# Attention with a relative bias, then routed experts: one PSUM ring for bias and scores, and a new order of the work

## The chip, the cores and the metric

The kernel runs on one core of a Trainium2 chip. The metric is the device time of one execution in microseconds; before, the median of three runs is 383.62 us (377.87, 383.62 and 387.02). Engines: PE (TensorE) multiplies matrices into PSUM, ACT (ScalarE) and DVE (VectorE) work on elements, POOL (GpSimd) and SP (SyncE) here mostly issue DMAs. [...]

## The reference

Eight batches, eight heads, 576 positions, head size 64; then eight experts over the 4608 resulting rows of 512.

```python
scores = scale * np.matmul(q, k.transpose(0, 1, 3, 2))
x = (psi_rel / psi_i)[..., None]          # psi_rel = log1p(|i - j|), psi_i = log1p(max(i, 1))
h = np.maximum(x @ w1 + b1, 0.0)          # hidden size 32
bias = h @ w2                             # one value for each head, i and j
scores = scores + bias.transpose(2, 0, 1)[None, :, :, :]
attn = np.exp(scores - max); attn = attn / sum
x = np.matmul(attn, v)                    # rows of all heads side by side
for e in range(E):
    mask = domain_id == e
    out[mask] = np.maximum(x[mask] @ w1[e], 0.0) @ w2[e]
```

## The kernel before, in words

The kernel has three stages.

**Bias.** The bias is the same in every batch, so the exponential of it is computed once and kept in SBUF (`biasM`, `biasR`, `biasL`, `biasRL`), and the exponentials of the scores are multiplied by it. `_phase_bias` goes through nine groups of 16 hidden rows. `hidden(ib)` makes the rows `hr`, some on ACT (L205), the others on DVE (L208); `outputs(ib, hrl)` multiplies them by the second layer into a PSUM tile `eb` (L225, and L229 for the last 64 keys), and ACT takes the exponential (L241, L238, L248). The ninth group (ib 8) is for the last 64 queries. Between these the routing (`_phase_route`, a generator of small DVE instructions) and the first transposes of q and k are woven in.

**Attention.** `_Attention.run` goes through nine rounds of 21 units; round b computes the scores of batch b (`scores`: score matmuls L530, L536, L543, L552 into a PSUM tile `sc`; exponential on ACT, L556) and the sums over the values (`av`, L580 to L596, into `pu`) of batch b and of what is left of batch b - 1. `weight` multiplies by the bias on DVE (L567), `norm` divides (L610, L611; L623, L627 for the last 64 positions) and scatters rows to `x_dram` on POOL's queue, at positions that the routing gave. `PLAN` is the written order: A is `av`, N `norm`, W `weight`, T and D transposes of q and k for the next batch on PE (L480) and their copy by DVE (L505), V the values with a column of ones; a prime means the batch before. PE, DVE and ACT keep the written order (`manual_schedule`); DMAs on POOL's queue keep theirs through `G.issue`.

PSUM: two banks `tr` for transposes and the routing, for the whole kernel; in the bias stage three `eb` tiles of two banks; in attention two `sc` tiles of two banks and one accumulator `pu` of two banks; with the experts two `hps` tiles of two banks and two `ops` tiles of one.

**Experts.** `_phase_moe`: for each expert the rows are fetched from `x_dram` by a transposing DMA (`fetch`, three tiles in turn), `first` computes the hidden layer (L781, relu on ACT, L813), `second` the output in five chunks of 128 rows (L757, copied by DVE, L760, and scattered by POOL, L761). The first 512 rows of expert 0 (`EARLY`) are fetched in the last attention round. Weights are loaded in 32 parts by POOL (L719): 17 during attention, and 15 one after each chunk. `_phase_overflow` is a loop over chunks that had no room in an expert's 640 rows; it stands behind everything and runs no time with these inputs.

## Time and profile before

| what | value |
|---|---|
| median of three runs | 383.62 us |
| span of the profiled execution | 383.4 us |
| PE busy over the span | 330.1 us (86%) |
| DVE busy | 238.8 us (62%) |
| ACT busy | 248.8 us (65%) |
| first score exponential | at 56.80 us |
| first matmul of the experts | at 229.16 us |
| issue of the last scatter | 373.92 to 374.90 us |

The shares over the whole span mix the three stages, so the stretches are to be read one by one. A row of a group gives line, engine, operation, output and input, shape and count, busy time and mean length of one, and then how long the engine had been idle before them and what ended it. "remote" stands where nothing that the profile shows ended an idle time. [...]

### The profile page before, as it was taken

How to read it: one execution, taken by the hardware profiler on the slowest of the kernel's cores; microseconds unless marked ns; L12 is line 12 of the kernel's file. 1: busy time of each engine (PE TensorE's matmuls, PEld its weight loads, DVE VectorE, ACT ScalarE, POOL GpSimd, SP SyncE). 2: the span in 40 equal slices, each digit the busy share in tenths (PEclk: the TensorE clock that was granted, in tenths of full speed). 3: DMA queues.
4: the chain of work that ended last, by engine and by line, in shares of the span. 5: the costliest groups of instructions: out<-in, count | busy, mean ns of one | idle time of the engine just before them, and what ended most of it. 6: DMA issues, size and time to landing. Idle time of an engine off the chain costs nothing. (4 is left out here: it accounts for less than half of the span.)

```text
span 383.4 us, 9399 instructions
## 1 busy us (share of the span) xinstructions
PE 330.1 (86%) x3938; PEld 216.2 (56%) x3938; DVE 238.8 (62%) x456; ACT 248.8 (65%) x303; POOL 177.3 (46%) x220
## 2 busy tenths in 40 slices
PE   1489997779898989989897779999999996999990
PEld 0378774546565665656574554665565644565630
DVE  7999968999899999999999762202122121212030
ACT  8999968789899989899989834242332402231500
POOL 9250006109486766676964513737451064233241
PEclk9999757999999999999999989999999998999996
DMA  5999977909999998979999933999999997021221
GB/s 87 179 172 370 374 276 98 146 0 129 130 150 152 130 169 106 181 103 200 132 210 227 229 76 82 200 238 205 237 206 231 185 181 224 28 93 56 77 89 39
DMA packets 90995, 61.30 MB, mean 160 GB/s; under 512 B 43461, under 2 KB 85189, under 8 KB 90952
## 3 DMA queue, kind: packets, MB, share of 16 engines
q0 software_dynamic: 59904, 45.12, 69.9%
q1 hardware_dynamic: 31048, 15.57, 17.0%
q8 instruction: 31, 0.51, 0.5%
q14 instruction: 12, 0.10, 0.1%
HBM read 61.93 MB, written 24.70 MB: 226 GB/s over the span
## 5 line engine op out<-in xcount | busy, mean ns | idle before, releaser
L556 ACT ACTIVATE e<-sc 128x1024 f16<-128x1024 f32 x168 | 152.8, 1012 | 16.2 <-PE sc L530 12.8
L760 DVE COPY res<-ops 128x512 f32<-128x512 f32 x40 | 27.7, 692 | 114.2 <-PE ops L757 108.2
L813 ACT ACTIVATE hT<-hps 128x640 f16<-128x640 f32 x56 | 39.4, 703 | 83.1 <-PE hps L781 77.8
L567 DVE TENSOR_TENSOR e<-e,biasM 128x2048 f16<-128x2048 f16 x64 | 71.8, 1151 | 1.8 <-ACT e L556 1.4
L757 PE MATMUL ops<-w,hT 128*128 128x512 f16 x320 | 70.5, 379 | 0.0
L761 POOL DMA_INDIRECT out_dram<-res,ids x40 | 39.7, 992 | 62.5 <-DVE res L760 48.5
L781 PE MATMUL hps<-xT,w 128*128 128x320 f16 x448 | 64.0, 304 | 3.0 <-ACT hT L813 3.0
L530 PE MATMUL sc<-qkT 64*128 64x512 f16 x256 | 49.9, 394 | 9.9 <-ACT e L556 8.0
L781 PEld LDWEIGHTS <-w 128*128 128x128 f16 x448 | 44.5, 99 | 22.4 <-issue 3.4
L757 PEld LDWEIGHTS <-hT 128*128 128x128 f16 x320 | 31.2, 98 | 36.5 <-ACT hT L793 0.3
L584 PE MATMUL pu<-vext,e 128*128 128x65 f16 x1024 | 50.1, 196 | 0.0
L641 POOL DMA_INDIRECT fire_x<-xt,posi x32 | 38.7, 1210 | 22.8 <-DMA last<-in_q_dram 10.3
L584 PEld LDWEIGHTS <-e 128*128 128x128 f16 x1024 | 44.4, 100 | 3.3 <-issue 2.4
L719 POOL DMA_DIRECT2D w<-in_moe_w_dram x32 | 28.1, 905 | 30.0 <-PE hps L781 18.6
L208 DVE TENSOR_SCALAR hr<-L,slope,nb 128x576 f16<-128x576 f16 x116 | 41.3, 450 | 0.0
L225 PE MATMUL eb<-W2BIG,hr 128*128 128x32 f16 x576 | 27.9, 193 | 13.1 <-DVE hr L208 9.4
L580 PE MATMUL pu<-vrag,e 128*128 128x130 f16 x128 | 29.2, 228 | 7.4 <-DVE xt L611 6.1
L225 PEld LDWEIGHTS <-hr 128*128 128x128 f16 x576 | 23.3, 116 | 17.6 <-DVE hr L208 14.4
L641 POOL DMA_INDIRECT fire_x<-xl,posi x8 | 13.3, 1667 | 39.3 <-DVE vext L477 18.6
L530 PEld LDWEIGHTS <-qkT 64*128 64x128 f16 x256 | 15.0, 93 | 25.4 <-issue 15.7
L580 PEld LDWEIGHTS <-e 128*128 128x128 f16 x128 | 12.6, 98 | 21.9 <-issue 10.1
L505 DVE COPY qkT<-pt 128x1024 f16<-128x1024 f16 x32 | 22.0, 688 | 4.3 <-PE pt L480 4.3
(124 smaller groups left out, 372.7 us busy)
## 6 DMA issues: line engine op xcount, KB each, us to landing
w<-in_moe_w_dram POOLq DMA_DIRECT2D x32, 512.0 KB
fire_x<-zero SPq DMA_DIRECT2D x1, 9252.0 KB
qn<-in_q_dram POOLq DMA_DIRECT2D x8, 512.0 KB
kn<-in_k_dram POOLq DMA_DIRECT2D x8, 512.0 KB
vst<-in_v_dram POOLq DMA_DIRECT2D x8, 512.0 KB
out_dram<-res,ids POOLq DMA_INDIRECT x40
last<-zero SPq DMA_DIRECT2D x2, 256.0 KB, 3.3
last<-in_q_dram POOLq DMA_DIRECT2D x16, 32.0 KB
```

The lines of the kernel that those rows point to most:

```text
L208: nc.vector.tensor_scalar(out=hr, in0=G.L4[:, c0: c0 + S], scalar1=G.slope[:, m: m + 1], scalar2=G.nb1[:], op0=AO.mult, op1=AO.max)
L225: nc.tensor.matmul(out=eb[:, lj, 32 * k16: 32 * k16 + 32], lhsT=rap(hr, jc, [[4, 128]]), rhs=G.W2BIG[:, 0:32], start=True, stop=True)
L530: mm(out=sc[:, h2, :], lhsT=self.qkT[b, p][hs[h2], 1, 128 * c: 128 * c + 128], rhs=self.qkT[b, p][hs[h2], 0, :], start=not raw, stop=True)
L556: nc.scalar.activation(out=ef[:, 0:n], in_=sf[:, 0:n], func=AF.Exp, bias=0.0, scale=0.125)
L567: self.nc.vector.tensor_tensor(out=job[0], in0=job[0], in1=job[1], op=AO.mult)
L580: mm(out=self.pu[:, c // 2, o: o + 130], lhsT=er[:, p % 2, 128 * c: 128 * c + 128], rhs=vr[:, p, :], start=True, stop=False, skip_group_ch ...
L584: mm(out=self.pu[:, c // 2, o + 65 * h2: o + 65 * h2 + 65], lhsT=self.e[b, ("m", p, j)][:, h2, 128 * c: 128 * c + 128], rhs=vx[:, 2 * p + ...
L641: inst = self.nc.gpsimd.indirect_dma_start(out=self.x_dram[:, :], out_offset=bass.IndirectOffsetOnAxis(ap=self.G.posi[0:n, c:c + 1], axis= ...
L757: nc.tensor.matmul(out=ops_, lhsT=hT[:, fc, t0: t0 + 128], rhs=G.w.w2(e, fc), start=(fc == 0), stop=(fc == 7))
L761: inst = nc.gpsimd.indirect_dma_start(out=out[:], out_offset=bass.IndirectOffsetOnAxis(ap=idx.bitcast(I32), axis=0), in_=res[:], in_offset ...
L781: nc.tensor.matmul(out=hps[:, i, 0:HC], lhsT=G.w.w1(e, dc, fc), rhs=xT[:, dc, HC * hf: HC * hf + HC], start=(dc == 0), stop=(dc == 3))
L813: nc.scalar.activation(out=hT[:, fc, :].rearrange("p (a b) -> p a b", a=2), in_=first(e, xT, ((fc, 0), (fc, 1))), func=AF.Relu, bias=0.0, ...
```

## The change

One PSUM pool serves bias and attention: a ring of three tiles of two banks, used by the bias outputs, the scores and the pairs of transposes, and one tile `pu` of two banks, which the accumulators, the routing and the first transposes share. The transposes are made for two pairs of heads at once and copied by one instruction; one such copy, that of pairs 2 and 3 for batch 1, is done by ACT.

```diff
+            aps = att.enter_context(tc.tile_pool(name="aps", bufs=1, space=PS, reuse_waits="tile"))
+            G.ring = lambda: aps.tile([P, 2, 512], F32, tag="sc", name="sc", bufs=3)
+            G.acc = lambda: aps.tile([P, 2, 512], F32, tag="pu", name="pu", bufs=1)
...
-        sc = G.aps.tile([P, 2, 512], F32, tag="sc", name="sc", bufs=2)
+        sc = G.ring()
...
-            eb = fps.tile([P, 2, 512], F32, tag="eb", name="eb", bufs=3)
+            eb = G.ring()
...
+            o, i = t.rearrange("p i x f -> p i (x f)"), self.pt.pop((b, ps)).bitcast(F16)
+            if (b, ps) == (1, (2, 3)):
+                self.nc.scalar.copy(out=o, in_=i)
+            else:
+                self.nc.vector.tensor_copy(out=o, in_=i)
```

The plan by units is replaced by a list that orders units, sums, copies and multiplications alike. The bias becomes a generator: its last group's three outputs come after the score units `m03`, `m10` and `m11` of batch 0 (`LAST_ROWS`), and the unit `m00` of each batch is put into the round before.

```diff
+ROUND = """
+V r0 m01 N2' A40' A41' Wm31' Wm32' A42' A43' N4'
+m02 m03 A30' A31' Wr0 A32' A33' m10 m11 Wm01 N3'
+T01 Wm03 m12 m13 A00 A01 D01 m20 m21 Wm11 A02
+A03 Wm13 m22 N0 Wm21 m23 T23 r1 D23 A10 l0
+A11 l1 A12 A13 m30 x Wm23 m31 Wr1 N1 A20
+Wl1 A21 m00+ A22 D4 A23 m32 Wx m33
+""".split()
+LAST_ROWS = {"m03": 1, "m10": 1, "m11": 2}
```

In the bias the last 64 keys are written into both halves of the partitions by two matmuls for each row, of 16 columns each, so that one exponential on 128 partitions takes the place of two on 64. ACT makes three hidden rows in each group from the third on (before three or two), and one table set that holds the logarithm and the exponential is loaded at the start. `W2BIG` and `vrag` are cleared in front of the first slopes, and the second half of the logarithms (`rest`) comes after the first hidden rows.

```diff
-                    for h2 in range(2):
-                        o = G.biasR[64 * h2: 64 * h2 + 64, :, i0: i0 + 64] if ib < 8 else \
-                            G.biasRL[64 * h2: 64 * h2 + 64]
-                        nc.scalar.activation(out=o, in_=ebv[0:64, 0, h2::2, :],
-                                             func=AF.Exp, bias=0.0, scale=0.125)
+                        for h2 in range(2):
+                            nc.tensor.matmul(out=eb[64 * h2: 64 * h2 + 64, 0, 16 * k16: 16 * k16 + 16],
                                              lhsT=hr[:, 512:576],
+                                             rhs=rap(G.W2BIG, h2, [[2, 16]]), start=True, stop=True)
...
+                nc.scalar.activation(out=G.biasR[:, :, i0: i0 + 64] if ib < 8 else G.biasRL,
+                                     in_=eb[:, 0, 0:256].rearrange("p (i q) -> p q i", q=4),
+                                     func=AF.Exp, bias=0.0, scale=0.125)
...
+    nc.scalar.add_instruction(mybir.InstLoadActFuncSet(
+        name=nc.get_next_instruction_name(), engine=mybir.EngineType.Activation, act_func_set_id=LN_EXP,
+        ins=[], outs=[]))
```

The routing has some instructions fewer. The sums of the last 64 positions go to 128 partitions (two halves of a row each), so that one normalisation takes the place of two, and half rows are scattered; a row of `x_dram` is now two halves of 256 values, each with its own row number. Of a batch's row scatters, one goes out at once and three after later units (`send`); in the last two batches all four.

Weights: 19 parts are loaded during attention (four after one unit of batch 0), the other 13 in four bunches after experts 1 to 4. All experts' rows are fetched at the start of the expert stage, into eight tiles. PSUM of the experts is laid over the ring and the accumulator as four pools of two banks, with four `ops` tiles. The last pair of heads of the last batch accumulates in two ring tiles. The last chunk's output is made and copied in two halves, one by DVE and one by ACT. The overflow loop moves in front of the last expert, behind a condition.

```diff
+W_FIRST = {0: 4, 1: 2, 2: 2, 3: 2, 4: 1, 5: 1}
+W_LATE = {1: 3, 2: 4, 3: 3, 4: 3}
...
-    xTs = {e: fetch(e) for e in range(2)}
+    xTs = {e: fetch(e) for e in range(E)}
+    novf = None
     for e in range(E):
+        if e == E - 2:
+            novf = nc.values_load(G.novf[0:1, 0:1], min_val=0, max_val=NOVF)
+        if e == E - 1:
+            with tc.If(novf > 0):
+                _phase_overflow(tc, G, novf, moe_w1, moe_w2, x_dram, out)
...
         for kk in range(NCH):
-            if (e, kk) == (0, 2):
+            if (e, kk) == (0, 3):
                 first_rest(hT, xT)
             second(hT, 128 * kk, e, ids[:, kk, :])
-            G.w.load(1, G.w_late)
+        G.w.load(W_LATE.get(e, 0), G.w_first)
...
-    _phase_overflow(tc, G, moe_w1, moe_w2, x_dram, out)
...
+        ops, hps = cycle((0, 0, 2, 2)), cycle((1, 3))
+        G.ops = lambda: pools[next(ops)].tile([P, DM], F32, tag="ops", name="ops", bufs=2)
+        G.hps = lambda shape, dt=F32: pools[next(hps)].tile(shape, dt, tag="hps", name="hps")
...
+                if (b, p) == (B - 1, 3) and c % 2 == 0:
+                    self.pu = G.ring()
```

## Rows read from the trace of the kernel before

**Rows 1.** The first line of the page.
```profile
span 383.4 us, 9399 instructions
```

**Rows 2.** Stretches: us, length, busy time (instructions) by engine, clock, DMA share, GB/s.
```profile
0.00:56.80 56.80, 39.97 (x766) 34.09 (x766) 50.77 (x159) 51.47 (x74) 17.17 (x38) 0.87 1.06 246
56.80:81.50 24.70, 19.08 (x278) 12.35 (x277) 22.52 (x45) 19.30 (x21) 7.59 (x12) 0.87 0.74 95
81.50:204.00 122.50, 110.95 (x1793) 75.93 (x1791) 116.62 (x175) 114.39 (x127) 85.58 (x100) 1.00 1.00 145
204.00:225.60 21.60, 17.78 (x239) 11.90 (x238) 17.13 (x26) 19.14 (x22) 9.22 (x10) 0.92 0.99 195
225.60:229.20 3.60, 1.60 (x40) 1.38 (x38) 1.82 (x6) 0.00 (x0) 0.91 (x1) 1.00 0.36 81
229.20:374.90 145.70, 140.72 (x836) 80.50 (x832) 29.93 (x48) 44.48 (x61) 56.83 (x59) 0.99 0.77 155
```
The engines stand in the order PE, PEld, DVE, ACT, POOL.

**Rows 3.** The same view of two stretches with another granted clock.
```profile
42.60:59.50 16.90, 15.82 (x262) 12.25 (x264) 12.75 (x35) 13.50 (x21) 0.00 (x0) 0.50 0.76 274
...
322.50:325.80 3.30, 3.30 (x14) 1.88 (x13) 0.00 (x0) 1.41 (x2) 0.00 (x0) 0.50 0.34 72
```

**Rows 4.** Timeline of ACT and of DVE at the hand-over to attention: start, length, instruction.
```profile
53.74 2.21 ACT L248 ACTIVATE biasL<-eb 128x512 f16<-128x512 f32 x4 [2.95 <-PE eb L225]
...
58.35 0.69 DVE L505 COPY qkT<-pt 128x1024 f16<-128x1024 f16 x1 [4.15 <-PE pt L480]
```

**Rows 5.** Groups by line, 81.5 to 204 us: count, busy, mean ns, idle before.
```profile
L556 ACT ACTIVATE e<-sc 128x1024 f16<-128x1024 f32 (+1 forms) x127 | 115.4, 1013 | 8.1 <-PE sc L530 6.6 <-PE sc L536 0.6
...
L530 PE MATMUL sc<-qkT 64*128 64x512 f16 x192 | 36.5, 383 | 5.4 <-ACT e L556 4.3
```

**Rows 6.** Groups by line and shape, whole span.
```profile
L556 ACT ACTIVATE e<-sc 128x1024 f16<-128x1024 f32 x160 | 150.6, 1042 | 16.2 <-PE sc L530 12.8 <-PE sc L536 1.5 <-PE sc L543 0.7
...
L567 DVE TENSOR_TENSOR e<-e,biasM 128x2048 f16<-128x2048 f16 x56 | 67.0, 1217 | 1.8 <-ACT e L556 1.4 <-issue 0.2
...
L208 DVE TENSOR_SCALAR hr<-L,slope,nb 128x576 f16<-128x576 f16 x116 | 41.3, 450 | 0.0
...
L205 ACT ACTIVATE hr<-L,pb,slope 128x576 f16<-128x576 f16 x28 | 22.2, 858 | 1.0 <-DVE slope L169 0.8
L505 DVE COPY qkT<-pt 128x1024 f16<-128x1024 f16 x32 | 22.0, 688 | 4.3 <-PE pt L480 4.3
...
L627 DVE TENSOR_TENSOR xl<-pu,rz 64x256 f16<-64x256 f32 x16 | 6.7, 421 | 1.0
...
L238 ACT ACTIVATE biasR<-eb 64x256 f16<-64x256 f32 x16 | 6.0, 372 | 0.1
...
L241 ACT ACT_TABLE_LOAD x1 | 1.3, 1283 | 0.0
```

**Rows 7.** Timeline of PE at the hand-over to the experts.
```profile
227.00 0.23 PE L580 MATMUL pu<-vrag,e 128*128 128x130 f16 x1 [1.27 <-DVE xl L627]
```

**Rows 8.** Timeline of ACT, PE and POOL at the one hole among the experts.
```profile
321.60 0.70 ACT L813 ACTIVATE hT<-hps 128x640 f16<-128x640 f32 x1 [3.53 <-remote]
...
322.36 0.93 PE L781 MATMUL hps<-xT,w 128*128 128x320 f16 x3 [2.99 <-ACT hT L813]
...
307.62 0.79 POOL L719 DMA_DIRECT2D w<-in_moe_w_dram  x1 [18.61 <-PE hps L781]
```

**Rows 9.** The end: the last scatter, the last stretch, and two groups of the page.
```profile
373.92 0.98 POOL L761 DMA_INDIRECT out_dram<-res,ids  x1 [0.75 <-DVE res L760]
...
376.45:383.40 6.95, 0.00 (x0) 0.00 (x0) 0.00 (x0) 0.00 (x0) 0.00 (x0) 0.54 0.00 0
...
L760 DVE COPY res<-ops 128x512 f32<-128x512 f32 x40 | 27.7, 692 | 114.2 <-PE ops L757 108.2
L757 PE MATMUL ops<-w,hT 128*128 128x512 f16 x320 | 70.5, 379 | 0.0
```

**Rows 10.** Timeline of DVE at the start: the first hidden rows.
```profile
7.46 0.91 DVE L208 TENSOR_SCALAR hr<-L,slope,nb 128x576 f16<-128x576 f16 x2
```

More of the change, by code (lines that the diff above doesn't have):

```diff
@@ new lines, in _phase_bias, with rows @@
+    fsb = G.bias_pools.enter_context(tc.tile_pool(name="fsb", bufs=1, side="right"))
+    def rows(ib, hrl):
+        for k16 in range(16):
+            if ib < 8:
+                r, a = ib // 2, 16 * (ib % 2) + k16
+                m, c0 = 32 * r + a, C4 - (16 * a + r)
+            else:
+                m, c0 = 128 + k16, W4 + C1 - 4 * k16
+            hr = fsb.tile([P, S], F16, tag="hr", name="hr", bufs=34)
+            if k16 in ((2, 5, 8, 11, 14) if ib < 2 else (3, 8, 13) if ib < 8 else (2, 3, 4)):
+                nc.scalar.activation(out=hr, in_=G.L4[:, c0: c0 + S], func=AF.Relu,
+                                     bias=G.pb1[:], scale=G.slope[:, m: m + 1])
+            else:
+                nc.vector.tensor_scalar(out=hr, in0=G.L4[:, c0: c0 + S],
+                                        scalar1=G.slope[:, m: m + 1], scalar2=G.nb1[:],
+                                        op0=AO.mult, op1=AO.max)
+            hrl.append(hr)
+            if (ib, k16) == (0, 7):
+                G.slopes(16, NGR)
+            if (ib, k16) == (0, 14):
+                G.rest()
+            if (ib, k16) in ((1, 1), (1, 5), (1, 9), (2, 1), (2, 5)):
+                next(route)
+            if (ib, k16) in ((7, 3), (8, 1)):
+                at.take(0, (4,) if ib == 7 else (0, 1))
+            yield
@@ new lines, in _phase_bias @@
+    now = []
+    for _ in rows(0, now):
+        pass
+    for ib in range(9):
+        later = []
+        ahead = rows(ib + 1, later) if ib < 8 else iter(())
+        if ib == 1:
+            nc.vector.memset(G.zero.rearrange("p o (r d) -> p (o r) d", r=4)[:, :, HD:HW].bitcast(I32), PAD)
+            nc.sync.dma_start(out=x_dram.rearrange("(p c r) d -> p c (r d)", p=P, r=4),
+                              in_=G.zero.to_broadcast([P, NSLOT // P // 4, 4 * XW]))
+        for _ in range(6 if ib == 7 else 16):
+            next(ahead, None)
+        for _ in outputs(ib, now):
+            if ib == 8:
+                yield
+        for _ in ahead:
+            pass
+        if ib == 0:
+            next(route)
+        if ib in (5, 6):
+            at.transposes(0, (4,) if ib == 5 else (0, 1), G.acc())
+        if ib == 7:
+            yield
+        now = later
@@ L569, in av_begin @@
     def av_begin(self, b, p):
[L570 removed]
+        self.pu = self.G.acc()
     def av(self, b, p, c):
@@ L651, in start, with run @@
             self.load_v(b)
-            self.load_last(b)
+            for x in range(2):
+                self.load_last(b, x)
             self.load_vrag(b)
-    def run(self, route, late):
+    def run(self, bias, route, late):
+        G = self.G
         units = [("r", 0)] + [("m", p, c) for p in (0, 1) for c in range(4)] + [("r", 1)] + \
@@ new lines @@
+            at.run(bias, route, late)
+        G.msb = ctx.enter_context(tc.tile_pool(name="msb", bufs=1, reuse_waits="tile"))
+        pools = [ctx.enter_context(tc.tile_pool(name=f"mps{i}", bufs=1, space=PS, reuse_waits="tile"))
+                 for i in range(4)]
+        ops, hps = cycle((0, 0, 2, 2)), cycle((1, 3))
+        G.ops = lambda: pools[next(ops)].tile([P, DM], F32, tag="ops", name="ops", bufs=2)
+        G.hps = lambda shape, dt=F32: pools[next(hps)].tile(shape, dt, tag="hps", name="hps")
```

537 lines of the change are left out of this document (259 added, 278 removed).

## Prediction

> **What bounds the kernel now.** I read first the stretches [rows 2], since one share for the whole span would mix three kernels. In the bias stretch (0 to 56.8 us) ACT is busy 51.47 us and DVE 50.77; in the attention rounds between 81.5 and 204.0 ACT 114.39 and DVE 116.62 of 122.50, which is 93% and 95%; in the expert stretch (229.2 to 374.9) PE 140.72 of 145.70 and nothing else over half. So attention belongs to ACT and DVE together, and the experts to PE. The span is 383.4 us [rows 1]; the median of the three timed runs is 383.62, so the profiled execution stands for the middle run, and the sum is made against 383.4.
>
> Then I asked what ended the idle time. In the six middle rounds the exponentials waited 8.1 us in all, 6.6 of it for score matmuls, and the score matmuls waited 5.4 us, 4.3 of it for the exponentials: each waits for the other through a ring of two score tiles [rows 5]. [...] At the hand-over to the experts PE waited 1.27 us for DVE to empty the one accumulator [rows 7]. Inside the experts there is one hole: an ACT relu started 3.53 us late, released by nothing that its program waits for ("remote"), PE stood 2.99 us because of it [rows 8] and ran the next 3.30 us at clock 0.50 [rows 3].
>
> **The change part by part.**
>
> *Up to 81.5 us.* ACT loses one table load (1.283 us) and half of the biasR and biasRL exponentials, nine, each 0.372 us, as both halves of the partitions are now written by one [rows 6]: 9 x 0.372 = 3.3. It gains three hidden rows, 3 x 0.858 = 2.6, and one copy of a pair of q and k tiles, which no row shows on ACT: between two DVE copies (2 x 0.688 = 1.4) and two exponentials of the same shape (2 x 1.042 = 2.1); I take 1.9. Net 0.1 less: nothing. DVE loses three hidden rows (3 x 0.450 = 1.4), that same copy (1.4), one of two narrow normalisations (0.421) [rows 6], and some small routing instructions that I leave uncounted. Together 3.2 of 50.77 + 22.52 = 73.29 us. Its first row, at 7.46 us [rows 10], starts earlier because the clearings go in front of it, into a wait. So what can be gained is idle time: ACT was idle 56.80 - 51.47 = 5.3 and 24.70 - 19.30 = 5.4 us in the first two stretches [rows 2], 10.7 together, of which about 1 is before any instruction. With the last bias group cut into three and put among the first scores, ACT finds scores where it stood 2.95 us, and DVE multiplications where it stood 4.15. The bounds are 0 and 9.7. Against the upper one: PE at half clock sets the pace from 42.6 to 59.5, and the change gives it 16 more small matmuls in each of nine groups, into half the columns each; if they don't run beside one another, it is behind by that much. I take 5.5, a little over half, because at least the two waits of rows 4 have their work now.
>
> *Rounds two to seven.* The ring has three tiles instead of two, as the banks of the transposes join it, and the order of the work is new. A third tile lets PE be two exponentials ahead. What can go is ACT's 122.50 - 114.39 = 8.1 us; what bars it is DVE, which lost per round one narrow normalisation (0.421) and the fixed part of two copies that are merged into pairs (no row; nothing to 0.1 each). 6 x 0.5 = 3.0 leaves DVE at 113.6, just under ACT's 114.39. Two engines at 97% don't interlock perfectly; bounds 0 and 8.1, and I take the middle, 4.1.
>
> *The transposes in the ring.* Each pair now holds a ring tile until DVE has copied it. If DVE comes in time this costs nothing, the cover being the two exponentials (2 x 1.042 us) whose scores stand in the other tiles. If DVE is late, PE waits at the next score tile and then ACT. That is the slow rival below.
>
> *Last round and hand-over.* ACT idle in the last round is 21.60 - 19.14 = 2.5, and PE's wait for the accumulator 1.27 [rows 2, 7]. The last pair of heads now accumulates in ring tiles, one for each half, so PE needs no emptied accumulator: I take that wait whole, 1.3, and 1.0, under half, from the round: 2.3. The bounds are 0 and the whole hand-over stretch but its matmuls (3.60 - 1.60 = 2.0) with the round's 2.5: 4.5.
>
> *The experts.* All rows are fetched at the start into eight tiles, and the weights that came one by one on POOL's queue between the scatters now come in four bunches into tiles that have long been read. POOL's queue, where a weight load stood 18.61 us before its tile came free and had the scatters behind it [rows 8], isn't blocked any more. The hole of rows 8 costs 2.99 us idle and half of the 3.30 us at half clock, 1.6: 4.6 together. It fell in the time when late transposes, a weight load and the held-back scatters were all on the DMA queues; these move away, so I take all of it (bounds 0 and 4.6).
>
> *The overflow loop moves in front of the last expert, behind a condition.* PE must read a register, see its own matmuls done, and branch. Below: one matmul's length, 0.379 us [rows 9]. Above: a stall like that of rows 8, 4.6 us. Waiting only for itself is nearest to the first; I take 0.7. POOL waits there for the scatters before it, with the last expert's scatters behind it, but these have first to wait for that expert's hidden layer, 64 matmuls.
>
> *The end.* Half of the last output tile is copied by ACT beside DVE's half: 0.3 of the 0.692 us. The last scatter's issue ends at 373.92 + 0.98 = 374.90; 1.55 us later the last 6.95 us begin, in which neither an engine nor DMA is busy [rows 9]. The loop's exit is in these, and the program's own end. Bounds for the loop's part are 0 and the 1.55; I take 0.4.
>
> Sum: 383.4 - 5.5 - 4.1 - 2.3 - 4.6 + 0.7 - 0.3 - 0.4 = 366.9, so 367.
>
> **The rivals.**
>
> *Attention doesn't move.* DVE at 95% and the half clock keep the rounds as they are, and only the two waits of rows 4 count, of them the smaller: 383.4 - 3.0 - 1.3 - 4.6 + 0.7 - 0.7 = 374.5. For it: DVE is busier than ACT in rows 2. Against it: ACT's waits name score matmuls, not DVE [rows 5].
>
> *The hole stays.* If ACT stood for a reason of its own and not for traffic, it stands again: 367 + 4.6 = 371.5. For it: no DMA is named at 321.60 as what released it [rows 8]. Against it: it is one hole in eight experts, PE being busy 140.72 of 145.70 us [rows 2].
>
> *The condition stalls PE.* If the branch makes PE wait for other engines or for its next instructions, the last expert starts late, as in rows 8, with half clock behind it: 367 - 0.7 + 4.6 = 370.8. [...] No row of before shows a branch with matmuls behind it.
>
> *Slower: the transposes block the ring.* In seven rounds two pairs each hold a tile until DVE copies it. DVE's queue is in order; if a multiplication (1.217 us) and the copy itself (about 1.4) are still to come when the other tiles are empty, ACT stands up to 2.6 us each time. At 2.0 us it is 14 x 2.0 = 28: 367 + 28 = 395. It decides from 16.4 / 14 = 1.2 us a time. For it: in all 32 copies DVE waited 4.3 us for transposes [rows 6], nearly all at once [rows 4], so the transposes mostly stand ready before DVE comes. Against it: in the new order one multiplication, or none, is written between a pair's transposes and its copy.
>
> *Everything fits.* ACT never waits: 383.4 - 9.7 - 8.1 - 4.5 - 4.6 + 0.4 - 0.3 - 1.5 = 355.1.
>
> **How the numbers follow.** Forecast 0.38, everything fits 0.07, attention doesn't move 0.25, the hole stays 0.13, the condition stalls 0.08, the ring blocks 0.09. The three timed runs of before lie 2.4% apart, so some 2% is what a measurement can tell from no change; that puts the border at 375.9. Faster: 0.38 + 0.07 + nine tenths of 0.21 + half of 0.25 = 0.76; slower 0.09; the rest, 0.15, the same. The range leaves out the blocked ring and the full fit and reaches over the unmoved attention by its own spread of 3 us: 359 to 378.
>
> **What would show it.** ACT's busy share of the middle rounds over 95% and its wait for scores under 5 us (right), or unchanged (attention didn't move). First exponential near 50 us, among biasL ones. No idle of ACT over 1 us in the attention hand-over. PE at one stretch from the first expert to the last, with under 1 us before the last one. In the ring, PE's score matmuls named as waiting for DVE copies would mean that the slow rival is at work. I am wrong altogether if PE's clock stays at 0.50 into the first full round, for then PE sets the pace there.

## The result: 355 us, below the range

The new kernel takes 354.67 us (median of six runs, 353.72 to 356.30) against 377.91 us (six runs of the kernel before beside it, 376.43 to 387.02). The ratio is 0.941, with a 95% interval of 0.938 to 0.944: 5.9% faster. Forecast was 367 in 359 to 378. The direction was right; the size was too small, and the time lies below the range, 0.4 us from the rival "everything fits". The kernel before took either 376.4 to 378.0 us or 383.6 to 387.0 in these six runs (this ratio, like those below, goes by the shorter ones), and both of its profiles are of longer executions, so that a part of the difference between the profiles, in whichever stage, belongs to those executions and not to the change. A span is not a time, either: wherever a run has both, the time is 1.5 to 1.7 us above the span (356.3 against 354.7). The 383.4 that the prediction subtracts from is a span and belongs to a run of some 385 us, and its 367 stands for a time of about 368.5 (estimates from that difference).

The new kernel's page: the span, the busy shares, and PE's granted clock in 40 slices, in tenths of full speed.

```profile
span 354.7 us, 9924 instructions
PE 316.9 (89%) x4250; PEld 209.5 (59%) x4250; DVE 228.3 (64%) x425; ACT 245.0 (69%) x298; POOL 177.7 (50%) x223
PEclk9999998999999999999999999999999999999998
```

Its stretches, cut at the same events as [rows 2]: first score exponential, end of the first round, six middle rounds, last round, hand-over, experts, end. Columns: us, length, busy time of PE, PEld, DVE, ACT and POOL, granted clock, DMA share, GB/s.

```profile
0.00:50.66 50.66, 33.88 (x813) 29.80 (x814) 46.56 (x145) 46.39 (x63) 17.70 (x41) 1.00 1.10 269
50.66:76.00 25.34, 22.71 (x372) 15.28 (x372) 23.60 (x50) 22.99 (x28) 10.22 (x15) 0.93 1.22 167
76.00:188.10 112.10, 103.75 (x1908) 71.70 (x1908) 110.24 (x157) 112.07 (x127) 84.98 (x101) 1.00 1.14 167
188.10:206.80 18.70, 15.88 (x285) 10.85 (x284) 16.75 (x25) 18.64 (x21) 8.94 (x8) 1.00 0.75 149
206.80:208.45 1.65, 1.40 (x38) 1.27 (x38) 1.35 (x5) 0.04 (x1) 0.00 (x0) 1.00 0.86 165
208.45:348.30 139.85, 139.24 (x845) 80.60 (x841) 29.84 (x49) 44.54 (x61) 54.59 (x57) 1.00 0.81 153
348.30:354.70 6.40, 0.03 (x1) 0.00 (x0) 0.00 (x0) 0.37 (x1) 1.26 (x2) 0.83 0.17 66
```

ACT is now busy 112.07 of the 112.10 us of the middle rounds; before it was 114.39 of 122.50. In the experts PE is busy 139.24 of 139.85 us. Neither has idle time left to fill there.

The groups of 82 to 188 us say the same by waits (count, busy us, mean ns, idle before; [rows 5] are those of before). The exponentials' 8.1 us of idle time are 0.0, the score matmuls' 5.4 us are 2.8:

```profile
L582 ACT ACTIVATE e<-sc 128x1024 f16<-128x1024 f32 x115 | 107.1, 1088 | 0.0
L593 DVE TENSOR_TENSOR e<-e,biasM 128x2048 f16<-128x2048 f16 x39 | 47.0, 1216 | 0.0
L554 PE MATMUL sc<-qkT 64*128 64x512 f16 x182 | 32.8, 384 | 2.8 <-ACT e L582 1.7 <-DMA vrag<-in_v_dram 0.9
L606 PE MATMUL pu<-vrag,e 128*128 128x130 f16 x92 | 20.5, 223 | 1.4 <-DVE xl L652 1.4
```

Length of each stretch in us, from the start and end times of the exponentials and of the experts' matmuls (the end of a round is that of its last exponential). All but the first and the third are experiments below; those on the experts' hole have a table of their own.

| kernel | to first exponential | first round | six middle rounds | last round | hand-over | experts | end | span |
|---|---|---|---|---|---|---|---|---|
| before, [rows 1 to 9] | 56.8 | 24.8 | 122.5 | 21.5 | 3.6 | 143.8 | 10.5 | 383.4 |
| before_again | 56.9 | 24.6 | 118.2 | 19.3 | 5.9 | 145.0 | 10.5 | 380.4 |
| new | 50.7 | 25.3 | 112.1 | 18.8 | 1.6 | 139.9 | 6.4 | 354.7 |
| ring_of_two | 51.2 | 29.6 | 136.7 | 20.3 | 1.9 | 139.4 | 6.4 | 385.5 |
| old_order | 51.3 | 26.0 | 126.5 | 18.8 | 2.5 | 139.3 | 6.4 | 370.8 |
| old_order_ring_of_two | 51.5 | 31.0 | 143.1 | 19.1 | 2.3 | 141.4 | 6.4 | 394.8 |
| own_transposes | 50.9 | 29.0 | 122.3 | 20.3 | 2.5 | 139.3 | 6.4 | 370.7 |
| old_order_own_transposes | 51.6 | 28.7 | 127.1 | 19.1 | 2.4 | 139.4 | 6.4 | 374.8 |
| loop_at_end | 51.8 | 24.3 | 112.0 | 18.8 | 1.6 | 139.6 | 9.5 | 357.5 |
| before_loop_moved | 57.0 | 24.6 | 117.6 | 19.3 | 6.3 | 147.8 | 7.6 | 380.1 |
| exp_twice | 50.6 | 24.7 | 114.1 | 19.0 | 1.4 | 139.5 | 6.4 | 355.8 |
| norm_twice | 51.2 | 24.1 | 114.5 | 19.1 | 1.6 | 140.3 | 6.4 | 357.2 |
| bias_first | 57.1 | 23.7 | 112.7 | 18.8 | 1.9 | 139.9 | 6.4 | 360.4 |
| after_again | 51.0 | 24.2 | 112.0 | 18.8 | 1.6 | 139.9 | 6.4 | 353.8 |

### The profile page after: what moved, and what is told of

It reads as the page before. It is cut to its first block, busy times and chain, and to the rows that moved or that the text cites. A ratio compares the mean times of both kernels' runs of the same rounds, so it can differ in the third digit from the quotient of the medians.

```text
span 354.7 us, 9924 instructions
## 1 busy us (share of the span) xinstructions
PE 316.9 (89%) x4250; PEld 209.5 (59%) x4250; DVE 228.3 (64%) x425; ACT 245.0 (69%) x298; POOL 177.7 (50%) x223
## 3 DMA queue, kind: packets, MB, share of 16 engines
q1 hardware_dynamic: 31416, 15.61, 19.6%
## 4 chain that ended last, share of the span: by engine, by line
issue 14%; DMA 12%; PE 8%; POOL 6%; DVE 5%; ACT 2%; SPq 2%; POOLq 1%; DVEq 0%
DMA w<-in_moe_w_dram 6%; POOL out_dram L820 5%; DMA out_dram<-res,ids 4%; PE ops L814 3%; PE hps L844 2%; DVE e L593 2%; ACT e L582 2%; PE hps L854 2%; DMA ids<-fire_x 1%; SPq L832 1%; POOL w L773 1%; DMA xA<-fire_x 1%; DVE xt L637 1%; POOLq L1031 0%; DVE res L817 0%
## 5 line engine op out<-in xcount | busy, mean ns | idle before, releaser
L582 ACT ACTIVATE e<-sc 128x1024 f16<-128x1024 f32 x168 | 150.2, 1060 | 2.6 <-PE sc L554 2.5
L817 DVE COPY res<-ops 128x512 f32<-128x512 f32 (+1 forms) x40 | 27.4, 685 | 109.5 <-PE ops L814 108.4
L814 PE MATMUL ops<-w,hT 128*128 128x512 f16 (+1 forms) x328 | 70.6, 374 | 0.0
L610 PE MATMUL pu<-vext,e 128*128 128x65 f16 x992 | 45.8, 194 | 0.1
L610 PEld LDWEIGHTS <-e 128*128 128x128 f16 x1024 | 42.6, 98 | 1.4 <-DVE e L593 0.6
L239 PE MATMUL sc<-W2BIG,hr 128*128 128x32 f16 x576 | 25.6, 193 | 12.7 <-DVE hr L218 11.0
L606 PE MATMUL pu<-vrag,e 128*128 128x130 f16 x124 | 27.6, 223 | 1.7 <-DVE xl L652 1.7
L554 PEld LDWEIGHTS <-qkT 64*128 64x128 f16 x256 | 11.8, 94 | 22.9 <-issue 17.8
L215 ACT ACTIVATE hr<-L,pb,slope 128x576 f16<-128x576 f16 x31 | 24.5, 864 | 0.7 <-DMA pb<-in_b_dram 0.7
L466 POOL DMA_DIRECT2D qn<-in_q_dram x8 | 7.9, 986 | 30.7 <-PE pu L495 28.9
L672 POOL DMA_INDIRECT fire_x<-xl,posl x8 | 10.8, 1345 | 23.2 <-DVE e L593 10.3
```

Of the source, the lines that this page charges most:

```text
L239: nc.tensor.matmul(out=eb[:, lj, 32 * k16: 32 * k16 + 32], lhsT=rap(hr, jc, [[4, 128]]), rhs=G.W2BIG[:, 0:32], start=True, stop=True)
L554: mm(out=sc[:, h2, :], lhsT=self.qkT[b, p][hs[h2], 1, 128 * c: 128 * c + 128], rhs=self.qkT[b, p][hs[h2], 0, :], start=not raw, stop=True)
L582: nc.scalar.activation(out=ef[:, 0:n], in_=sf[:, 0:n], func=AF.Exp, bias=0.0, scale=0.125)
L610: mm(out=self.pu[:, c // 2, o + 65 * h2: o + 65 * h2 + 65], lhsT=self.e[b, ("m", p, j)][:, h2, 128 * c: 128 * c + 128], rhs=vx[:, 2 * p + ...
L672: inst = self.nc.gpsimd.indirect_dma_start(out=out, out_offset=bass.IndirectOffsetOnAxis(ap=at, axis=0), in_=x, in_offset=None)
L814: nc.tensor.matmul(out=ops_[:, d0: d1], lhsT=hT[:, fc, t0: t0 + 128], rhs=G.w.w2(e, fc)[:, d0: d1], start=(fc == 0), stop=(fc == 7))
```

## The experiments

**How far two executions of one kernel differ.** Both kernels were run once more, unchanged.

> The kernel before, unchanged, profiled once more. If the hole in the experts (ACT stands 3.53 us at 321.60, PE 2.99 us, then 3.30 us at half clock) belongs to the kernel's traffic, it stands at the same place again, some 93 us after the experts' first matmul, and POOL again waits about 18.6 us ahead of it. If it comes from outside the program's order, it is gone or somewhere else, and the span is 4 to 5 us shorter, about 379. The half clock from 42.6 to 59.5 us comes back if PE's own work there asks for it.

> The new kernel unchanged, once more. If its rounds have settled, the six middle rounds take 111.9 to 112.2 us again and the stretch from the first expert matmul to the last 139.3 to 140.3; only the first round moves, by the 3.4 us of half clock that the first profile had at 58.9 us. The median is 354 to 355.5 us.

Measured: the kernel before 382.87 us in four runs (377.21 to 385.59), the new one 355.81 (354.43 to 357.53). The new kernel's stretches repeat to 0.3 us but for the first round, which is 1.1 us longer in the first profile; PE's clock was granted at 0.51 there for 3.5 us from 58.9 us on. The kernel before does not repeat: its middle rounds took 118.2 us instead of 122.5, while PE now waited for rows from memory at the experts, which it had not done at all in the first profile. PE's waits of before_again, 204 to 380 us (waiting, waited for, us in total, times, longest):

```profile
PE hps L781 <- DMA xT<-fire_x: 3.7, 2, 2.8
PE hps L791 <- DMA xA<-fire_x: 2.0, 1, 2.0
```

So the hole of [rows 8] is not at one place: it was 2.99 us at a relu in one execution and 5.7 us of late rows in the other. The middle rounds and the last one together were 6.4 us shorter in the second execution, and 3.6 us of that was given back at the hand-over and in the experts, where rows were not there yet. Why the rounds settle at 20.4 us in one execution and at 19.6 in another stays open. The half clock from 42 to 59 us came back (0.50 from 44 to 56 us).

**The order and the ring.** Four kernels take one or both back: two score tiles in place of three, with the bias keeping a third tile to itself, and the old order. In the last two, a tile of their own holds the pairs of transposes, so that the scores have two tiles as before.

```diff
-            G.ring = lambda: aps.tile([P, 2, 512], F32, tag="sc", name="sc", bufs=3)
+            G.ring = lambda: aps.tile([P, 2, 512], F32, tag="sc", name="sc", bufs=2)     # ring_of_two
...
-V r0 m01 N2' A40' A41' Wm31' Wm32' A42' A43' N4'
-m02 m03 A30' A31' Wr0 A32' A33' m10 m11 Wm01 N3'
...
+r0 A40' m00 A41' A42' Wr0 m01 A43' N4' V m02 m03 A30' Wm01                           # old_order
+m10 A31' A32' Wm03 m11 A33' N3' m12 T01 Wm11 D01 m13 A00 A01
...
-                        self.transposes(b + 1, ps, self.G.ring())
+                        self.transposes(b + 1, ps, self.G.own())                       # own_transposes
```

> The new kernel with two score tiles in attention instead of three; the bias keeps a third tile of its own, and the order of the work is the new one. If the third tile is what shortened the rounds, the six middle rounds lose all of their gain: 112.2 us become about 120 to 122, and the total is 355 + 8 to 10 = 363 to 365. If the order is what did it, the middle rounds stay at 113 to 114 and the total at 356 to 357. If both are needed, it is over 360 here and over 360 with the old order too.

> The new kernel with the order of units, sums, copies and multiplications that the kernel before had, three tiles in the ring. If the order is what shortened the rounds, the six middle rounds go back from 112.2 to about 120 to 122 us and the total to 363 to 366. If the third tile did it, they stay at 113 to 115 and the total at 356 to 358.

> Both taken back: the order of before and two score tiles, in the new kernel. The pairs of transposes still stand in the score ring. If order and tiles are all that shortened the rounds, the middle rounds take about 122 us as before and the total is about 365 plus what the rest of the rounds loses; if transposes in the ring cost something that the third tile hid, they take more than 122.5 us, and ACT's waits lie behind the units that follow T01 and T23.

> The new kernel in its new order, with two score tiles and one tile of two banks that only the pairs of transposes use (in the bias it is the third tile). Ring of two gave 136.7 us for the six middle rounds, the new kernel 112.1. If all of that 24.6 us is the transposes that stand in the score ring, the rounds come back to 112 to 114 us here and the total to 354 to 358: the third tile only makes room for transposes. If the scores need three tiles of their own, the rounds stay at 118 to 122, as in the kernel before, and the total is 361 to 365.

> As own_transposes, with the order of the kernel before. Two executions of the kernel before had 122.5 and 118.2 us in the middle rounds, old_order with three tiles in the ring 126.5. If order and place of the transposes are all that counts, this has 117 to 122 us, and old_order's 126.5 is 5 to 9 us that the transposes in the ring cost even with three tiles. If the smaller changes of the rounds (pairs copied at once, one narrow normalisation) gain by themselves, it comes under 117.

Measured, medians in us (the first three ran on one chip, where the kernel before took 376.6 to 386.4 us, the last two on another, where it took 376.5 to 386.3; 354.67 is the result above):

| | transposes in a ring of three | in a ring of two | own tile, two score tiles |
|---|---|---|---|
| new order | 354.67 | 387.17 | 373.20 |
| old order | 373.63 | 394.58 | 377.48 |

None of the three theories had the sizes. Both are needed, and the tile is worth more than I gave it: with scores and transposes in two tiles the new order is slower than the kernel before, whose transposes have tiles of their own (ratio 1.026, 1.022 to 1.031), and without the new order the third tile gains 1% (0.990, 0.986 to 0.994), all of it outside the rounds, which take 126.5 us there, longer than in either profile of before. The slow rival of the prediction is real, and it is what one sees in ring_of_two. Its waits from 82 to 200 us:

```profile
ACT e L582 <- PE sc L554: 8.2, 22, 0.7
ACT e L582 <- PE sc L560: 4.0, 5, 0.8
...
PE sc L554 <- DVE qkT L529: 5.0, 5, 1.0
...
PE sc L567 <- DVE qkT L529: 2.3, 5, 0.5
...
DVE rzl L651 <- PE pu L623: 7.4, 6, 1.2
```

PE's score matmuls wait for the DVE copy of the transposes, L529, up to 1.0 us each time, ACT then waits for the scores, and DVE for the sums: the wait goes round all three. With three tiles no wait for L529 is left. A tile of their own for the transposes takes 14.4 of the 24.6 us out of the middle rounds (136.7 to 122.3), the same tile put into the ring, for scores and transposes alike, the other 10.2. In own_transposes the groups of 82 to 188 us show the stall that [rows 5] have, ACT and PE waiting for each other through two tiles:

```profile
L582 ACT ACTIVATE e<-sc 128x1024 f16<-128x1024 f32 x105 | 100.0, 1036 | 5.2 <-PE sc L554 3.1 <-PE sc L560 1.0
L554 PE MATMUL sc<-qkT 64*128 64x512 f16 x168 | 31.9, 383 | 9.5 <-ACT e L582 8.1 <-DVE qkTl L520 1.0
```

With the old order and three tiles it is another wait: DVE copies and divides late, and PE waits for the accumulator and for the exponentials. PE's and DVE's waits of old_order, 82 to 200 us:

```profile
PE pu L605 <- DVE xt L636: 7.9, 6, 1.3
PE sc L553 <- ACT e L581: 6.7, 6, 1.1
...
DVE e L592 <- ACT e L581: 9.4, 17, 0.6
```

old_order_own_transposes missed my figure (117 to 122) by 5 us: with transposes in pairs, the old order is worse in the rounds (127.1) than the kernel before was with single ones (117.6 to 122.5 in three profiles). So the smaller changes of the rounds, the pairs of transposes and the one narrow normalisation among them, gain nothing there by themselves; which of them costs the 5 us was not tried.

**Which engine bounds the rounds.** Two small additions, neither of which changes the output: the exponential of unit x is done twice in exp_twice, the division of the last 64 positions in norm_twice.

```diff
-        nc.scalar.activation(out=ef[:, 0:n], in_=sf[:, 0:n], func=AF.Exp, bias=0.0, scale=0.125)
+        for _ in range(2 if u[0] == "x" else 1):                                        # exp_twice
+            nc.scalar.activation(out=ef[:, 0:n], in_=sf[:, 0:n], func=AF.Exp, bias=0.0, scale=0.125)
...
+            for _ in range(2):                                                          # norm_twice
+                nc.vector.tensor_tensor(
```

> The new kernel with the exponential of the last 64 queries on the last 64 keys (unit x, 256 columns) done twice, which adds some 0.37 us of ACT to each batch and changes nothing else. If ACT alone sets the pace of a round (18.7 us), each round is 0.3 to 0.4 us longer: the six middle rounds 114 to 114.5 us, the total 2.5 to 3 us more, 357 to 357.7. If rounds are set by the order in which PE, ACT and DVE hand over, with slack on each, under 1 us: 355.

> The new kernel with the normalisation of the last 64 positions done twice in each batch, which adds about 0.42 us of DVE to a round and changes nothing else. DVE is busy 110.3 of 112.2 us in the six middle rounds, so 0.3 us a round is free. If ACT alone sets the pace, the rounds stay at 18.7 us and the total within 0.5 us of the new kernel's. If DVE is a second bound, each round takes 0.2 to 0.4 us more: 113.5 to 114.5 us in the middle, 356 to 358 in all.

Measured: 358.32 and 358.94 us; a middle round takes 19.02 us with the exponential and 19.14 with the division, against 18.67. ACT is a bound, as expected. DVE is one too, and not by its busy time: it had 0.3 us a round free and got 0.42 us more, and the round grew by 0.47. The middle rounds took what I had expected, at the upper end with the division (114.1 and 114.5 us), while both totals came out 0.6 to 0.9 us above the ranges that I had given. The row that shows why is PE's wait for the one accumulator, 1.4 us in the new kernel (L606 above) and here, 76 to 188 us:

```profile
PE pu L606 <- DVE xl L653: 4.0, 6, 0.7
```

The division empties the accumulator, PE's next sums and, behind them in its queue, the scores wait for it, and ACT then waited 1.1 us for the scores.

**The last bias group among the scores.**

```diff
-        next(bias)
+        for _ in bias:
+            pass
```

> The new kernel with all nine bias groups in front of the first scores, as before. If the last group among the scores is what shortened the stretch up to the end of the first round (81.6 us before, 74.4 to 76.0 now), the end of the first round goes back by 3 to 5 us, to about 79, and the total to 357 to 360. If the shorter hidden rows, exponentials and copies did it, it stays under 77 us, with only the first score exponential later by the 1.5 to 2.5 us of the last group's three exponentials.

Measured: 361.33 us, 5.5 us more than after_again on the same chip. The first round ends at 80.8 us (75.2 in after_again, 81.5 and 81.7 in the two profiles of before; I had expected about 79): the place of this group is nearly the whole gain up to there. With the group taken back, the fewer exponentials, the copy on ACT and the table loaded early leave 0.7 to 0.9 us. The wait of [rows 4], 2.95 us then, is back. ACT's waits of bias_first, 45 to 62 us:

```profile
ACT biasL L261 <- PE sc L239: 3.8, 1, 3.8
ACT biasM L254 <- PE sc L239: 1.4, 1, 1.4
```

**The last 64 keys in the old form.**

```diff
-                        for h2 in range(2):
-                            nc.tensor.matmul(out=eb[64 * h2: 64 * h2 + 64, 0, 16 * k16: 16 * k16 + 16],
...
+                        nc.tensor.matmul(out=eb[0:64, lj, 32 * k16: 32 * k16 + 32],
...
```

> The new kernel with the last 64 keys' bias in the old form: 16 matmuls of 32 columns into 64 partitions and two exponentials on 64 partitions for each group, instead of 32 matmuls of 16 columns and one exponential. Nine times 0.37 us of ACT come back: if ACT sets the pace of the bias, the first score exponential moves from 50.7 to 53 to 54 us and the total to 357 to 358; if DVE does, under 1 us. If the smaller matmuls are what kept PE at full clock, the clock falls to 0.50 at 42 us again and stays there to some 59 us, and the last bias group costs 1 to 3 us more.

Measured: 356.21 us (355.44 to 357.22); the first exponential stands at 51.1 us, the first round ends at 76.3. So the 3.3 us of ACT are not in the time up to the first exponential (50.7 and 51.0 us in the new kernel): ACT is not what the bias waits for. The clock does fall, but later than I thought. Three stretches of last_keys_in_64, and below them one of after_again:

```profile
40.00:44.00 4.00, 3.91 (x96) 3.75 (x95) 4.00 (x12) 3.96 (x7) 0.00 (x0) 1.00 1.10 351
44.00:48.00 4.00, 3.95 (x98) 3.63 (x94) 4.00 (x11) 3.96 (x7) 0.00 (x0) 1.00 1.12 355
...
52.00:56.00 4.00, 4.00 (x64) 2.67 (x63) 4.00 (x11) 3.17 (x5) 1.88 (x2) 0.54 0.41 34
```

```profile
40.00:44.00 4.00, 3.18 (x98) 3.04 (x98) 4.00 (x13) 4.00 (x6) 0.00 (x0) 1.00 1.11 354
```

With as many matmuls (96 and 98) PE is busy 3.91 us instead of 3.18. The new kernel's records say why: 284 of the 288 matmuls of 16 columns begin in twos, within 4 ns of each other, and from the first start of a group to the last its 32 matmuls take 0.82 us in seven of nine groups, as long as the 16 of 32 columns in the old form (0.82 us in seven of nine groups of the kernel before). So the pairs of 16 columns into two halves of the partitions do run beside one another, which was my doubt about them. In the one profile of the old form the clock is at 0.60 and 0.54 in the two stretches from 48 to 56 us, with little lost: the first round ends 0.3 us later than in the new kernel's first profile and 1.1 us later than in its second.

**The end.**

```diff
-        if e == E - 1:
-            with tc.If(novf > 0):
-                _phase_overflow(tc, G, novf, moe_w1, moe_w2, x_dram, out)
...
+    _phase_overflow(tc, G, novf, moe_w1, moe_w2, x_dram, out)      # loop_at_end; the reverse in before_loop_moved
```

> The new kernel with the overflow loop at the very end and no condition, as before. From the last matmul to the end of the span it took 10.5 us before and takes 6.4 now. If the loop's exit, which every engine has to leave after the last scatter has landed, is what POOL's closing drain (4.7 us before, 5.1 now) waited for, the end goes back to 10 to 10.5 us here and the total to 358 to 359. If the halves of the last output tile did it, the end stays under 7 us and the total at 355. PE's 0.30 us in front of the last expert goes away in both.

> The kernel before with nothing changed but the overflow loop, which stands in front of the last expert behind a condition. If the loop's place makes the end, from the last matmul it takes 6.5 to 7 us instead of 10.5, and the total is 3.5 to 4 us shorter than before: a ratio of 0.990. PE then waits 0.3 us in front of the last expert. If the condition stalls PE where POOL's queue is still full of scatters, the gain is eaten there.

Measured: 359.18 and 382.12 us. The four kernels make a square of the two edits; from the records of the trace, counted from the end of the last matmul (us):

| | loop at the end, whole copy | at the end, copy in halves | moved, whole | moved, in halves |
|---|---|---|---|---|
| kernel | before | loop_at_end | before_loop_moved | new |
| last scatter issued | 1.01 to 1.99 | 0.68 to 1.67 | 1.00 to 1.99 | 0.68 to 1.67 |
| POOL's closing drain starts | 4.98 | 4.32 | 0.77 | 0.45 |
| its length | 4.73 | 3.91 | 5.95 | 5.14 |
| end of the span | 10.52 | 9.50 | 7.55 | 6.41 |

The place of the loop is worth 3.0 to 3.1 us and the halves 1.0 to 1.1. Behind the loop POOL's closing drain starts 1.04 us after the last scatter has landed (at 3.28 us in loop_at_end); without it the drain begins beside that scatter. In before_loop_moved the 3 us did not arrive in the total, against what I had expected (a ratio of 0.990): it is slower than the kernel before, 1.014 (1.011 to 1.017). In its profile PE waited 6.7 us for late rows at the experts, which took 147.8 us. What made more rows late there isn't settled. PE's wait in front of the last expert is 0.3 us in every kernel that has the condition (0.39 in ring_of_two); in the new one:

```profile
PE hps L844 <- DMA out_dram<-res,ids: 0.3, 1, 0.3
```

**The hole in the experts.** Four kernels bring back the fetches of rows two experts ahead, the weights one after each chunk from expert 1 on, both, and both with the old number of early loads (one after each chunk of every expert).

```diff
-    xTs = {e: fetch(e) for e in range(E)}
+    xTs = {e: fetch(e) for e in range(2)}                       # fetch_in_turn: three tiles, and fetch(e + 2) ahead of the chunks
...
-        G.w.load(W_LATE.get(e, 0), G.w_first)
+            G.w.load(1 if e else 0, G.w_first)                  # loads_one_by_one
...
-W_FIRST = {0: 4, 1: 2, 2: 2, 3: 2, 4: 1, 5: 1}
+W_FIRST = {0: 1, 1: 1, 2: 1, 3: 1, 4: 1, 5: 1}                  # weights_as_before: four more in round 7
```

> The new kernel with the experts' rows fetched two experts ahead into three tiles in turn, as before, instead of all at the start into eight; the weights still come in four bunches. The kernel before, profiled twice, lost 2.99 us to a late relu in one execution and 2.8 and 0.9 us to rows that came late (PE named as waiting for the DMA into xT) in the other. If the late fetches are that hole, PE waits 2 to 4 us for xT in the middle of the experts here, the stretch from the first expert matmul to the last grows from 139.9 to 142 to 144 us, and the total to 357 to 359. If the hole is POOL's held-back queue, nothing is lost here: 355.

> The new kernel with the late weights issued one after each chunk from expert 1 on, instead of in four bunches; the rows are still all fetched at the start. If POOL's queue, held by a load whose tile isn't free yet, with the scatters behind it, makes the hole, POOL again shows a wait of over 10 us at a weight load and PE loses 2 to 5 us between the first expert and the last: 357 to 360. If the late fetches of rows were it, the experts stay at 139 to 140.5 us, however long POOL stands: 355.

> The new kernel with the rows fetched two experts ahead and the late weights one after each chunk, as before the change both. Each of the two alone brought PE at most 1.05 us of waiting for rows. If the hole needs both (a load that waits on POOL's queue and pushes later loads and scatters into the time of a fetch), PE loses 2 to 4 us in the middle of the experts here: 357 to 359. If not, the sum of the two: 354 to 356, and the hole of before comes from something else in the old expert stage.

> The new kernel with the experts' traffic as before: rows fetched two experts ahead into three tiles, 17 parts of the weights during attention (six singly, seven in round 6, four at the start of the last round), the other 15 one after each chunk from the first expert on. If the crowd of weight loads makes the transposing fetches late (median 21 us from issue to landing before, 6.2 now, in 60 us of the experts), PE waits 2 to 6 us for xT as in the two profiles before, the experts take 142 to 145 us and the total is 357 to 360. If the fetches land in time all the same, the hole belongs to something else that the change took away, and the total is 354 to 357.

> The new kernel with the late weights one after each chunk from expert 1 on, once more. If it is better than the new kernel (353.64 against 354.67 and 355.81 in other calls), its median is again under 354.2; if those were differences between chips, it lies between 354.2 and 356.

Measured: 355.85, 353.64, 356.59, 377.05 and 361.06 us. The last two ran on a chip that held the kernel before to 382 to 405 us and are compared with each other only. Both lie outside what I had expected for them, weights_as_before (357 to 360) by far. The experts' stretch in the profiles, the time that PE stood idle in it for over 0.25 us at once, and the longest of these idle times with what ended it (us):

| kernel | rows fetched | late loads | experts | PE idle | the longest |
|---|---|---|---|---|---|
| new; after_again | at the start | bunches | 139.9; 139.9 | 0.3; 0.3 | 0.3, the condition |
| fetch_in_turn | in turn | bunches | 140.8 | 1.4 | 1.05, rows (xT) |
| loads_one_by_one | at the start | one by one | 139.8 | 0.3 | 0.3, the condition |
| loads_one_by_one_again | at the start | one by one | 143.6 | 3.1 | 1.13 and 1.10, late relus |
| both_in_turn | in turn | one by one | 143.4 | 2.6 | 2.31, early rows (xA) |
| weights_as_before | in turn | one by one | 153.4 | 8.3 | 3.04, nothing named |
| before | in turn | one by one | 143.8 | 3.0 | 2.99, late relu |
| before_again | in turn | one by one | 145.0 | 3.7 | 2.81, rows (xT) |
| before_loop_moved | in turn | one by one | 147.8 | 4.5 | 3.78, rows (xT) |

POOL's held-back queue alone is not the hole. In loads_one_by_one it stands as long as in [rows 8], and PE loses nothing. POOL's wait and PE's longest one, 205 to 350 us:

```profile
POOL w L773 <- PE ops L814: 18.1, 2, 17.0
```

```profile
PE hps L844 <- PEq L872: 0.3, 1, 0.3
```

But the same kernel, run again on the other chip, lost 3.1 us, and with the picture of [rows 8]: relus of ACT that started late with nothing named ("remote"), and PE waiting for them. Its waits from 200 to 350 us:

```profile
ACT hT L882 <- remote: 1.5, 2, 0.8
...
PE hps L844 <- ACT hT L882: 1.6, 3, 1.1
```

No profile of a kernel with its loads in bunches has such a relu. Fetching in turn costs PE 1.05 us in fetch_in_turn, at the first expert. The 2.31 us of both_in_turn were for the early rows, whose fetch that edit leaves as it is; the clock was granted at 0.84 behind them, from 206.5 to 212 us. The median of both_in_turn is 0.8 us above that of after_again, on the same chip.

weights_as_before took 372.3 to 383.3 us in its four runs, against 359.5 to 362.2 for loads_one_by_one_again; the profile is of one of 379.2, so that what it shows need not hold for the other runs. PE's waits, 200 to 350 us:

```profile
PE hps L854 <- DMA xA<-fire_x: 6.4, 2, 5.6
PE ops L814 <- issue: 3.0, 1, 3.0
PE hps L844 <- DMA xT<-fire_x: 2.3, 1, 2.3
```

That looks like the picture of before: rows late at the hand-over and in the middle, and one stop of 3 us that no wait of the program explains. From 240 to 300 us before_again and the new kernel have 13 weight loads each, one behind the other from 238 us on in the former and in bunches with 9 to 15 us between them in the latter. How long the transposing fetches of rows then took from issue to landing (the median, last in the row) doesn't tell them apart. In before_again, in the new kernel (each fetch of half the columns) and in after_again:

```profile
xT<-fire_x SPq DMA_TRANSPOSE x4, 21.0
...
xT<-fire_x SPq DMA_TRANSPOSE x6, 6.2
...
xT<-fire_x SPq DMA_TRANSPOSE x8, 17.4
```

after_again waited for none of its rows all the same: the last fetch of all rows at the start is issued early (at 261 us in the new kernel, the last expert begins at 331).

So the cause of the hole stays open. Every profile that lost 3 us or more in the experts has its loads one by one, and those in bunches lost 2.1 at most; but loads_one_by_one lost nothing with them on one chip, so something else must come to it. How much of the 12 us between the last two kernels belonged to their chip, and what the plan of the loads would cost with all rows fetched early, was not tried. loads_one_by_one is no better version than the new kernel: on the second chip its ratio to the kernel before is 0.938 (0.932 to 0.944), where the new kernel has 0.941.

## Why the prediction fell short, step by step

The sum subtracted 16.5 us from 383.4. The two profiles differ by 28.7, the medians by 23.2. Of the 12.2 us that the sum missed against the profile, 6.3 are in rounds two to seven, 3.4 at the end, 2.4 in the last round and the hand-over and 0.2 in the first stretch.

- *Up to 81.5 us*: taken 5.5, measured 5.7 (81.65 to 75.99), and for the reason given: the two waits of rows 4 got work. The instructions that I counted on ACT don't show (last_keys_in_64). Right.
- *Rounds two to seven*: taken 4.1, measured 10.4 against the profile ahead of the prediction and 6.1 against before_again. Two steps failed. First, one execution was taken for the kernel ("the profiled execution stands for the middle run"): 4.2 us of the 122.5 are not in the second profile. Second, the upper bound of 8.1 us, ACT's idle time, was no bound. 115 exponentials of 1.088 us (L582 above) would be 125.1 us, and they stand in 106: an exponential that follows another at once begins 0.90 to 0.92 us after it (126 of 144 in the new kernel), though its record is 1.02 us or longer. So each idle gap costs its own length and some 0.1 us of overlap beside (an estimate from these two): the middle rounds of before and of before_again have 24 gaps each, of 8.1 and 3.6 us in all, and the new kernel, with one of 0.03 us, is 10.4 and 6.1 us shorter. My half of the bound was then half of too little. "Two engines at 97% don't interlock perfectly" was wrong as well: with a third tile and an order made for it ACT is busy 99.97%. Merging two copies, for which I had no row, saved 0.16 us a pair: one of the new kernel takes 1.218 us (L529), two of before took 2 x 0.688 [rows 6].
- *Transposes in the ring*: taken at nothing; with three tiles no wait for their copy is left, in a ring of two they cost 14.4 us of the middle rounds. My reason, one multiplication or none before each copy, was not the cover; the third tile is.
- *Last round and hand-over*: taken 2.3, measured 4.7 (25.05 to 20.38), a little over my upper bound of 4.5. The hand-over's part, 2.0, is that bound's; of the last round's 2.7, only 0.6 is left against before_again, so this too was mostly one execution taken for the kernel.
- *Experts' hole*: taken 4.6, with the condition's 0.7 against it, net 3.9; measured 3.9 (143.75 to 139.89). The size came out, by luck in part, as the second profile of before has 145.0 and the hole at other places. The cause is not shown: POOL's held-back queue alone is not it (loads_one_by_one), and neither the loads one by one nor the fetches in turn bring it back each time. The condition cost PE 0.30 us, less than the lower bound of 0.4.
- *The end*: taken 0.7, measured 4.1. This step failed worst in proportion. I saw that in [rows 9] neither an engine nor DMA was busy for 6.95 us and took it as the program's own end, bounding the loop's part by 1.55 us. A closing drain of 4.7 us was in it, and with the loop moved it starts 3.9 to 4.2 us earlier; what I should have asked is what it waited for.

Of the rivals, "attention doesn't move" and "the hole stays" fell with the new kernel's first profile, and "the condition stalls PE" with the 0.30 us: in the new kernel's records PE's branch stands at 326.50 us, 0.36 us long, while the matmuls in front of it still run, the last of them to 330.53, and the next expert's first matmul begins at 330.83. That PE waits there for its next instructions no run shows. "The transposes block the ring" is true of ring_of_two. "Everything fits" gave 355.1 by bounds of which the middle rounds' and the end's were too small and the first stretch's too large (9.7 against 5.7); that its total came so near is luck, as these errors cancel. Its chance, 0.07, was set too low even so, because I gave each stage its own doubt although one cause, the ring and the order together, stood behind the waits of all rounds.

## What to carry to other kernels

An engine's idle time is not the most that can be saved, where its instructions overlap when they follow each other at once (here the exponentials, 0.90 to 0.92 us apart with records of 1.02 us and more): divide the stretch by the count and compare the step with the step where nothing waits. When transposes or other short-lived tiles move into a ring, the ring's depth and the written order are one edit: here the new order with one tile less was slower than the kernel before, and the third tile in the old order gained 1%. Where nothing seems busy at the end, ask what the closing steps wait for, and profile the kernel before twice before subtracting from it.

## What the hardware showed that was not expected

- Exponentials of 128x1024 that follow each other begin 0.90 to 0.92 us apart in 126 of 144 cases in the new kernel, while each record is 1.02 to 1.24 us long.
- Matmuls of 16 columns in pairs, into two halves of the partitions, ran beside one another in the new kernel: 284 of 288 began in twos, within 4 ns, and 32 take 0.82 us in seven of nine groups, as 16 of 32 columns do.
- POOL's closing drain took 3.9 to 4.7 us behind the landed scatter and 5.1 to 5.9 us beside it; after the loop it began 3.9 to 4.2 us later than without.
- The time of a transposing fetch from issue to landing differs between two executions of one kernel: 6.2 and 17.4 us (medians, 240 to 300 us) in the new one.
- PE's clock was granted at 0.50 from 44 to 56 us in both profiles of the kernel before and in that of before_loop_moved, after PE had been busy 3.70 to 3.75 and 4.00 us in the two stretches of 4 us from 32 to 40. In the new kernel, with the last keys in pairs of half-sized matmuls, it stayed at 1.00 there, after 2.96 and 3.91 us in the same two stretches of its first profile.
